# mLSTM cell and multiplicative FFN: the sign of high words on ScalarE, transposes of k, q and y moved from TensorE to VectorE and DRAM

## The chip, the cores and the metric

The kernel runs on one core of a Trainium2 chip. The metric is the device time of one execution in microseconds (us). The engines are PE (TensorE; PEld is its weight load, which overlaps the matmuls), DVE (VectorE), ACT (ScalarE), POOL (GpSimd) and SP (SyncE, which here only issues DMAs). [...]

## The reference, cut to what matters

For every batch (4) and head (8) an mLSTM cell runs over 768 time steps with a head size of 40; its output, 3072 tokens by 320, goes through a feed-forward block.

```python
for t in range(S):                                   # S = 768
    m_new  = max(f_gate + m, i_gate)
    C = exp(f_gate + m - m_new) * C + exp(i_gate - m_new) * outer(v, k)
    n = exp(f_gate + m - m_new) * n + exp(i_gate - m_new) * k
    y[t] = sigmoid(o_gate) * (C @ q) / max(abs(n @ q), 1)
x = y as (3072, 320)
out = (((x @ w1) * (x @ w2)) @ w3) @ w_out           # w1, w2: 320 x 1024; w3: 1024 x 1024; w_out: 1024 x 320
```

The four weights arrive as 64-bit floats, the rest as 32-bit floats. The kernel itself turns each weight into 32 bits, from its low and its high word.

## The kernel before, in words

**Units.** Time is cut into pieces of 128 steps, and a unit is one such piece of one batch: 6 x 4 = 24 units. Four units (one of each batch) are a group of 512 tokens of the feed-forward block. The main loop (L568) has 30 steps, s = 0 to 29. Step s runs the cell of unit s (its scores and its addition to the state, together with the output of unit s-1: `quarter_work`, L308), and beside it the feed-forward work of earlier units: "ups" (x @ w1 times x @ w2, `up` L521 and `up_rest` L534), "downs" (`ffn_out`, L544) from step 17 on, and in steps 10 to 17 one piece each of w3 @ w_out (`w3_mm`, L248), which is folded into one matrix.

**Weights.** `fetch` loads 64-bit words into `raw`; ScalarE scales the high word (`scale`, L171); VectorE puts the 32-bit number together in five instructions (`to_f32`, L175, lines 184 to 188), of which L185 fetches the sign. For w3 a sixth instruction turns the tile (L237). 34 such conversions are spread over steps 0 to 15 (`n_cvt`, L563).

**Transposes.** TensorE needs k, q and y with the token along the free dimension. For units 0 to 16 `turn` (L281) does k and q with eight 128x128 transposes on TensorE (tile `pt`) and two ScalarE copies out of PSUM (L295). For units 17 to 23 `load_turned` (L125) loads k and q in another arrangement, eight DMAs in all, into `turned_in`, one pair of buffers in the tile `gates`, and VectorE turns them by two 32x32-block transposes (L287). Units of that kind load no plain q. For y, `twice` (L385) has GpSimd copy the last 64 columns once more, and `x_trans` (L388) does three transposes on TensorE (tile `px`) and one ScalarE copy into `xT` (L396).

**Order.** All matmuls and transposes are held in the order in which they are recorded (`in_order`, L82). In a step this is: `pt`, `px` of unit s-3, `wp`, the downs, the ups, their rest (64-row matmuls), and then the cell: output of unit s-1, state product, and last the scores of unit s, which need kT and qT of unit s. On the other engines the tile framework's scheduler orders the instructions at build time; `tc.issue_after` marks some as not to be placed before another. PSUM has four rotating banks (`mps`, L75) for all but the cell, and the cell has one tile, which a step can write again only when VectorE has read it (`outputs`, L362, lines 366 and 370).

## Time and profile before

| | before |
|---|---|
| time, median of 3 runs | 486.15 us (486.0 to 486.35) |
| profiled execution, its own time | 483.81 us |
| span of that execution | 482.1 us |
| mean granted TensorE clock | 0.982 |
| busy: PE, DVE, ACT, POOL | 454.6, 259.9, 146.8, 86.6 us |
| DMA | 45.72 MB, mean 95 GB/s |

The span runs from the first to the last instruction; 1.7 us of the execution lie around it. In the timeline a step can be told by the tile `cell`: steps 12 to 15 take 16.77 us each, step 17 (one piece of w3 @ w_out and two downs) 24.51 us, and steps 18 to 23 20.2 us each. Durations of matmuls are modelled, so for TensorE the starts are read, and not the ends.

### The profile page before, as it was taken

What the parts mean: (1) busy time and instruction counts of PE and PEld (TensorE: products, weight loads), DVE (VectorE), ACT (ScalarE), POOL (GpSimd) and SP (SyncE); (2) the same over time, 40 slices, a digit from 0 to 9 for tenths busy, and PEclk for the clock granted to TensorE, in tenths of its full rate; (3) what the DMA queues carried; (4) which work ended last, traced back from release to release, by engine and by line L of the source; (5) the groups of instructions that cost most, each with busy time, mean ns of one, the idle gap of its engine ahead of it and who ended that gap; (6) DMA issues with size and microseconds to landing.
All of it is one profiled execution on the core that took longest, in us unless ns stands there. A gap on an engine that the chain in (4) does not pass through costs nothing.

```text
span 482.1 us, 12855 instructions
## 1 busy us (share of the span) xinstructions
PE 454.6 (94%) x5402; PEld 365.6 (76%) x5402; DVE 259.9 (54%) x526; ACT 146.8 (30%) x399; POOL 86.6 (18%) x165
## 2 busy tenths in 40 slices
PE   3868999799999999999999999999999998999997
PEld 2757877678878888788878787787877877778864
DVE  7797798989886968887451533614325033011110
ACT  3644545443442353354331321311101111011011
POOL 5442322520220322213220211201000000000000
PEclk9995999989999999999999999999999999999999
DMA  8999977599698656433350623324020000000001
GB/s 183 166 166 200 194 139 137 114 203 191 125 189 135 127 127 148 94 66 57 77 132 15 141 57 96 66 81 110 3 82 16 14 27 3 29 14 16 1 14 41
DMA packets 116185, 45.72 MB, mean 95 GB/s; under 512 B 96736, under 2 KB 107168, under 8 KB 116128
## 3 DMA queue, kind: packets, MB, share of 16 engines
q1 hardware_dynamic: 112528, 40.88, 43.4%
q10 hardware_dynamic: 3600, 4.03, 2.4%
q8 instruction: 42, 0.69, 0.6%
q14 instruction: 15, 0.12, 0.1%
HBM read 40.86 MB, written 4.03 MB: 93 GB/s over the span
## 4 chain that ended last, share of the span: by engine, by line
PE 81%; issue 7%; DVE 7%; POOL 2%; DMA 1%; ACT 1%; ACTq 0%; SPq 0%; POOLq 0%; DVEq 0%
PE pa L90 23%; PE po L90 22%; PE pb L90 16%; PE cell L90 9%; PE wp L90 7%; PE pt L93 2%; DVE h L370 1%; PE px L93 1%; PE ub L90 1%; POOL pw L278 1%; DVE o_in L380 1%; DVE h L366 1%; DMA raw<-in_moe_w_out_dram 1%; POOL state L305 1%; DMA gates<-in_i_gate_dram 1%
## 5 line engine op out<-in xcount | busy, mean ns | idle before, releaser
L542 DVE TENSOR_TENSOR ab<-pb,a_sb 128x512 f32<-128x512 f32 x48 | 33.0, 689 | 162.1 <-ACT a_sb L541 162.0
L90 PE MATMUL po<-w3o,ab 128*128 128x320 f32 x384 | 105.4, 433 | 1.3 <-DVE h L370 1.3
L90 PEld LDWEIGHTS po<-w3o,ab 128*128 128x128 f32 x384 | 72.2, 190 | 30.7 <-issue 1.5
L90 PE MATMUL pa<-xT,w 128*128 128x256 f32 x384 | 92.5, 384 | 0.9 <-ACT xT L396 0.6
L90 PE MATMUL pb<-xT,w 128*128 128x256 f32 x384 | 90.8, 379 | 0.0
L90 PEld LDWEIGHTS pa<-xT,w 128*128 128x128 f32 x384 | 73.3, 193 | 14.1 <-ACT xT L396 1.0
L90 PEld LDWEIGHTS pb<-xT,w 128*128 128x128 f32 x384 | 72.9, 190 | 10.3 <-DVE ab L542 0.4
L541 ACT ACTIVATE a_sb<-pa 128x512 f32<-128x512 f32 x48 | 28.6, 595 | 151.3 <-PE pb L90 151.3
L90 PE MATMUL pa<-xT,wr 64*64 64x256 f32 x384 | 47.0, 383 | 0.0
L90 PE MATMUL pb<-xT,wr 64*64 64x256 f32 x384 | 47.0, 383 | 0.0
L305 POOL TENSOR_TENSOR state<-state,decay 128x164 f32<-128x164 f32 x40 | 19.6, 495 | 146.9 <-PE cell L90 91.5
L278 POOL TENSOR_SCALAR_AFFINE_SELECT pw<-pw 64x512 f32<-64x512 f32 x48 | 35.5, 740 | 47.8 <-ACT pw L276 46.2
L276 ACT ACTIVATE pw<-pw,aT 128x64 f32<-128x64 f32 x160 | 40.7, 338 | 8.1 <-DMA pw<-U_d 8.1
L90 PEld LDWEIGHTS pa<-xT,wr 64*64 64x64 f32 x384 | 25.8, 133 | 16.8 <-issue 7.8
L90 PE MATMUL wp<-wo,w3T 128*128 128x320 f32 x128 | 35.9, 433 | 0.1
L90 PEld LDWEIGHTS cell<-vbuf,pw 64*64 64x64 f32 x768 | 27.5, 141 | 6.1 <-issue 1.9
L549 ACT COPY o_sb<-po 128x320 f32<-128x320 f32 x24 | 10.2, 423 | 67.9 <-PE po L90 63.6
L90 PEld LDWEIGHTS wp<-wo,w3T 128*128 128x128 f32 x128 | 23.7, 190 | 9.1 <-PE px L93 0.3
L90 PE MATMUL cell<-vbuf,pw 64*64 64x41 f32 x768 | 27.4, 231 | 2.2 <-issue 1.3
L386 POOL COPY y<-y 128x64 f32<-128x64 f32 x24 | 7.1, 296 | 108.1 <-DVE y L382 104.2
L90 PEld LDWEIGHTS pb<-xT,wr 64*64 64x64 f32 x384 | 25.8, 133 | 0.0
L346 DVE TENSOR_TENSOR pw<-cell,pw 128x512 f32<-128x512 f32 x24 | 16.4, 684 | 15.3 <-PE cell L90 15.2
(89 smaller groups left out, 514.0 us busy)
## 6 DMA issues: line engine op xcount, KB each, us to landing
raw<-in_moe_w_dram SPq DMA_DIRECT2D x64, 128.0 KB, 3.2
pw<-U_d SPq DMA_DIRECT2D x40, 128.0 KB, 3.6
kbuf<-in_k_dram SPq DMA_DIRECT2D x24, 160.0 KB, 4.4
vbuf<-in_v_dram SPq DMA_DIRECT2D x24, 160.0 KB, 5.0
o_in<-in_o_gate_dram SPq DMA_DIRECT2D x24, 160.0 KB, 4.0
out_dram<-o_sb ACTq DMA_DIRECT2D x24, 160.0 KB, 1.9
raw<-in_moe_w_dram SPq DMA_DIRECT2D x7, 512.0 KB, 5.9
qbuf<-in_q_dram SPq DMA_DIRECT2D x17, 160.0 KB, 4.8
```

The costliest lines, as they stand in the source:

```text
L90: in_order(nc.tensor.matmul(out, lhsT=lhsT, rhs=rhs, start=start, stop=stop))
L93: in_order(nc.tensor.transpose(out, in_, ident[0:n, 0:n]))
L276: nc.scalar.activation(out=pw[:, h, :], in_=src[:, h, :], func=AF.Exp, bias=aT[:, c, b * H + h:b * H + h + 1])
L278: nc.gpsimd.affine_select(out=pw[r], in_=pw[r], compare_op=OP.is_ge, fill=0.0, base=0, pattern=[[0, H], [1, L]], channel_multiplier=-1)
L305: nc.gpsimd.tensor_tensor(out=new, in0=old, op=OP.mult, in1=decay[:, b * NP:(b + 1) * NP, 2 * c + x:2 * c + x + 1] .to_broadcast([P, NP, D1]))
L346: first_read = nc.vector.tensor_tensor(out=pv, in0=ss, in1=pv, op=OP.mult)
L366: nc.vector.tensor_tensor(out=h.rearrange("p (n two) d -> p two n d", two=2), in0=pi, in1=gT[:, c, hs].rearrange("p (n two) -> p two n", t ...
L370: nc.vector.tensor_tensor(out=h[r], in0=ph[x], in1=h[r], op=OP.add)
L386: nc.gpsimd.tensor_copy(out=y_t[n][:, DM:DM + REM], in_=y_t[n][:, KF * P:DM])
L541: nc.scalar.mul(out=a_sb, in_=pa, mul=UP ** -2)
L542: nc.vector.tensor_tensor(out=ab_t[gr][j][:, fs[0]:fs[-1] + 1, t0:t0 + a_sb.shape[-1]], in0=pb, in1=a_sb, op=OP.mult)
L549: nc.scalar.copy(out=o_sb, in_=po)
```

## The change

Three things are changed.

1. The sign of a weight's high word is brought to its place by ScalarE: the scaling becomes a parametric ReLU with a slope of 2^32 for negative numbers, so that the shift by three on VectorE leaves the sign bit set or clear, and L185 goes.
2. `N_DVE` is 10 in place of 17: k and q of units 10 to 16, too, are loaded by `load_turned` and turned by VectorE.
3. From unit 15 on (`NY`; the sixteenth unit) y is sent to a DRAM tile by four DMAs (`send`), read back in another arrangement by four more (`get_back`), and turned by one VectorE transpose (`x_turn`). `twice` and `x_trans` are not called for these nine units. All the DMAs are issued by SP.

```diff
-    N_DVE = 17
+    N_DVE = 10
...
+    NY = 15
     KC = KF + 1
+    y_d = [dram.tile([P, 4, KC, 32], FP, name=f"y_d{n}") if n >= NY else None for n in range(NU)]
...
     def scale(raw):
         hi = raw[:, :, 1].bitcast(FP)
-        nc.scalar.mul(out=hi, in_=hi, mul=2.0 ** -111)
+        nc.scalar.activation(out=hi, in_=hi, func=AF.Prelu, scale=2.0 ** -111, alpha=2.0 ** 32)
...
         V.tensor_scalar(out=t, in0=hi, scalar1=3, scalar2=None, op0=OP.logical_shift_left)
-        V.scalar_tensor_tensor(out=t, in0=hi, scalar=0x80000000, in1=t, op0=OP.bitwise_and, op1=OP.bitwise_or)
         V.tensor_scalar(out=r, in0=t, scalar1=0xFF800000, scalar2=None, op0=OP.bitwise_and)
...
+    def send(n):
+        y = y_t.pop(n)
+        for cc in range(KF):
+            nc.sync.dma_start(out=y_d[n][:, :, cc, :], in_=y[:, cc * P:(cc + 1) * P].rearrange("t (i c) -> t i c", c=32))
+        for i in range(0, 4, 2):
+            nc.sync.dma_start(out=y_d[n][:, i:i + 2, KF, :], in_=y[:, KF * P:DM].rearrange("t (i c) -> t i c", c=32))
+    back_t = {}
+    def get_back(n):
+        back_t[n] = sb.tile([P, 4, KC, 32], FP, name="yb", tag="yb", bufs=1)
+        for i in range(4):
+            nc.sync.dma_start(out=back_t[n][32 * i:32 * (i + 1)].rearrange("r m k c -> r m (k c)"),
+                              in_=y_d[n][:, i].rearrange("(m r) k c -> r m (k c)", r=32))
+    def x_turn(n):
+        gr, j = divmod(n, GT)
+        if j == 0:
+            x_t[gr] = ffn.tile([128, KC, TG], FP, name="xT", tag="xT")
+        nc.vector.transpose(out=x_t[gr][:, :, j * P:(j + 1) * P].rearrange("c k (m r) -> c k m r", r=32),
+                            in_=back_t.pop(n).rearrange("r m k c -> r k m c"))
...
-        if 0 <= s - 2 < NU:
+        if NY <= s - 2 < NU:
+            send(s - 2)
+        elif 0 <= s - 2 < NY:
             twice(s - 2)
         if N_DVE <= s + 1 < NU:
             load_turned(s + 1)
-        while turned < min(s - 2, NU):
+        if NY <= s - 2 < NU:
+            get_back(s - 2)
+        while turned < min(s - 2, NY):
             x_trans(turned)
             turned += 1
...
-        if len(now) == 1 and turned == s - 2 < NU:
+        if len(now) == 1 and turned == s - 2 < NY:
...
         with tc.issue_after(gated.ins) if gated else nullcontext():
+            if NY <= s - 2 < NU:
+                x_turn(s - 2)
             if N_DVE <= s + 1 < NU:
                 turn(s + 1)
```

## The prediction

> **What bounds the kernel now.** First the page's slices: where an engine is full, and at what TensorE clock.

> ```profile
> PE   3868999799999999999999999999999998999997
> DVE  7797798989886968887451533614325033011110
> PEclk9995999989999999999999999999999999999999
> ```

> TensorE is full from slice 8 (97 us) to the end. Before that it has holes, VectorE is at eight tenths, and the clock dips twice. Then the stretches, step by step (columns: length, busy PE, PEld, DVE, ACT, POOL, clock, DMA share, GB/s):

> ```profile
> 157.33:174.10 16.77, 16.77 (x220) 13.81 (x221) 13.69 (x28) 6.93 (x20) 3.56 (x6) 1.00 0.58 119
> 241.19:265.70 24.51, 24.51 (x244) 19.02 (x245) 7.53 (x15) 5.45 (x15) 3.24 (x7) 1.00 0.31 72
> 33.80:35.20 1.40, 0.04 (x4) 0.00 (x0) 1.30 (x4) 0.69 (x1) 0.24 (x1) 0.98 1.04 109
> 35.20:36.70 1.50, 0.00 (x0) 0.00 (x0) 1.35 (x2) 0.00 (x0) 0.00 (x0) 0.50 0.87 122
> 96.70:100.20 3.50, 3.19 (x9) 2.46 (x9) 3.24 (x9) 2.90 (x11) 0.00 (x0) 0.53 1.27 170
> ```

> Step 12 (first line) has no TensorE idle time, so what is taken from TensorE there is won in full, provided that nothing new makes it wait. The last three: where TensorE idles for a few us, its clock halves. Then the chain that ended last (start, length):

> ```profile
> 174.10 1.02 PE pt L93 x8
> 175.45 4.31 PE wp L90 x16
> 241.19 0.48 PE px L93 x3
> ```

> The transposes are on it. Last the timelines of VectorE and TensorE around the end of step 17, where k and q are already turned by VectorE, and three waits:

> ```profile
> 246.16 1.11 DVE L287 STREAM_TRANSPOSE kT<-gates 128x512 f32<-128x512 f32 x1
> 247.11 1.09 DVE L287 STREAM_TRANSPOSE qT<-gates 128x512 f32<-128x512 f32 x1
> 263.19 0.69 DVE L542 TENSOR_TENSOR ab<-pb,a_sb 128x512 f32<-128x512 f32 x1 [14.99 <-ACT a_sb L541]
> 264.06 0.69 DVE L542 TENSOR_TENSOR ab<-pb,a_sb 128x512 f32<-128x512 f32 x1 [0.17 <-ACT a_sb L541]
> 264.95 0.26 PE L90 MATMUL cell<-qT,kT 40*64 40x64 f32 x2
> 265.63 0.55 PE L93 MATMUL px<-ident,y 128*128 128x128 f32 x3
> 266.01 1.24 PE L90 MATMUL po<-w3o,ab 128*128 128x320 f32 x4
> 95.82 0.66 PE L93 MATMUL pt<-ident,qbuf 128*128 128x128 f32 x4 [2.57 <-DVE ab L542]
> 407.92 4.28 PE L90 MATMUL po<-w3o,ab 128*128 128x320 f32 x15 [1.29 <-DVE h L370]
> ```

> The reader is to see that step 17 turns k and q at its start (246 us), 17 us before the scores want them at 264.95, and that the second `ab` ends only 0.2 us before the scores start.

> [...] the transpose at 95.82 waited 2.57 us behind an `ab` that stood behind conversions. [...] The trace agrees on the half (0.50) and on the grid (the changes at 35.2, 96.7 and 100.2 us lie whole multiples of 3.42 us apart), but the drop at 35.2 us came only 1.4 us into a gap[...]. [...] the trace has a single load, of 1283 ns, and the changed program also holds one.

> **The change part by part.** "Step" is the loop's s; the sums are made on the profiled execution (span 482.1, time 483.81 us).

> *Sign.* 34 instructions of L185 leave VectorE: 32 of 668 ns in the mean and 2 of 852, 23.1 us together (0.69 on a wide tile, 0.49 on w_out's narrow ones). They pay only where TensorE waits for VectorE. Up to step 5 it doesn't: VectorE idles 0.7 to 1.1 us before each L346, for the cell. In step 5 VectorE is late by 2.7 us (L346 starts at 68.78, its scores end at 66.1); two conversions fewer by 0.69 each bring L346 to 67.40, and step 6 loses another 0.69 + 0.49 and its lateness. What was late there on TensorE goes: 0.17 us (bank of `pb`, step 6) and 1.07 us (`pt` of q at 80.23). In step 7 the cell then ends 1.24 us earlier, at 91.35; L346 runs at 78.4, `y` ends 5.45 later as before (80.69 to 86.14), at 83.85, three conversions take 8.96 less 3 sign instructions (0.84 + 0.49 + 0.49, and gaps) = 7.05 and end at 90.9. The changed order puts three quarters of a fourth conversion (1.2 us) ahead of the first `ab`: it ends at 92.75, the second at 93.85, where `pa` had to wait until 97.18. That is 3.3 us. The wait before it shrinks from 2.57 to 0.8 us, so the halved clock at 96.7 should not come: `pa` took 3.38 where it takes 1.73, 1.65 us more. Together **-4.9** (between -2, if stalls in loads take the place of the conversions, and -6.5, if step 9 gains too). The activation itself stays at its 0.63 us.

> *k and q of units 10 to 16.* Off TensorE go eight `pt` a step: step 17 without its downs is 24.51 - 8.61 = 15.90, against 16.77: 0.87 a step. ScalarE loses two copies of 0.59, off the path. Added are 2 transposes of 1.1 us on VectorE, eight DMAs less one q load on SP. VectorE has room in sum: 13.69 - 2 x 0.67 + 2.2 = 14.6 us a step. What decides is where they stand. The built program lists for steps 11 to 15

> ```
> ...  ab  ab  kT<-gates  qT<-gates  pw<-cell (L346)
> ```

> and for step 10 `ab ab`, a whole w3 conversion, then kT, qT; in step 16 qT stands before the second `ab`, and from step 17 on both follow `y`, as at 246.16. The `ab`s wait for this step's ups, so kT and qT can't start before them; the scores, the last matmuls of the same step, wait for both; behind the scores stands the whole next step. Priced on step 17: second `ab` at 264.06, kT 0.60 later (the spacing at which VectorE follows a 0.69 us instruction), qT 0.95 after it and 1.10 long: 266.71, and 0.05 for the semaphore. The scores would start at 264.95: **1.81 us of stall a step**. Steps 12 to 15: -0.87 + 1.81 = +0.94, four times = +3.8. Step 11: 17.71 against 17.85 (it held 0.85 us of idle issue): -0.1. Step 10: the conversion (0.45 + 0.46 + 0.73 + 0.73 + 0.64 = 3.0) comes on top: 15.90 + 4.8 = 20.7 against 17.07: +3.6. Step 16: -0.9. Together **+6.4**. The turned loads come in time: each is issued after the last turn, some 16 us before the next, and lands in 2.5 us.

> *Clock.* The gap of 4.8 us in step 10 must halve the clock for about a window: half of 3.42 = +1.7. The gaps of 1.81 us, behind 1.7 us of small cell matmuls, look like the window that dropped at 35.2 us[...]. The trace shows no such gap; between 0 and 5 x 1.7 I take 2.5 x 1.7: **+4.2**.

> *y of units 15 to 23.* Off TensorE go three `px` in steps 18 to 26: 266.01 - 265.63 = 0.38 each. In step 25 the first down also waits for `h` until 407.92, since `px` takes the free bank before it; without `px` the down takes that bank, at 406.08: 1.84. Sum 8 x 0.38 + 1.84 = **-4.9**. Added: one VectorE transpose of some 0.9 us (between L237's 0.71 and L287's 1.1; not seen with this shape), beside 13 idle us a step; and eight DMAs a unit. x of a unit is wanted one step or more after it is turned; `send` plus `get_back` take perhaps 6 us after `y`, and x_turn stands a step (20 us) later. So nothing; if they took more than 20 us, kT and qT behind x_turn would stall the scores.

> Sum: -4.9 + 6.4 + 1.7 + 4.2 - 4.9 = **+2.5**: a profile of some 486.3 us, and 486.15 + 2.5 = **488.7 us** for the median, which lies 2.3 above this profiled execution.

> **The rivals.**
> 1. *The clock holds.* A gap of 1.3 us at 406.6 and one of 1.17 at 61.0 left it at 1.00. If 1.81 does too: +2.5 - 4.2 = -1.7, and without step 10's, -3.4: **483.6**, faster. It decides at two dips in five steps: with none or one dip the sum is negative or zero. Chance 0.21.
> 2. *Every step dips*, or two windows each: 5 x 1.7 and more, +6.7 and beyond: **493**. Chance 0.16.
> 3. *A turned load is late.* SP also carries eight `raw` DMAs a step (9.0 us in step 12) and the turned loads now wait for VectorE in the midst of them. Late by 2 us in six steps: **500**. Against it: 16 us of room. Chance 0.07.
> 4. *The turns don't stall* (the scores find them ready): -4.9 - 7.3 - 4.9 = -17, **469**. Against it: the listed order. Chance 0.05.

> **How the numbers follow.** The forecast has 0.51. Its own range is 486 to 491; with rivals 1 and 2, and the bounds of the sign's gain, 483 to 495.5; some 0.14 stay outside. Against 486.15 a measurement tells 0.2% (1 us) from nothing: faster, rival 1 mostly, rival 4: 0.22; same, the forecast's low end: 0.15; slower: 0.63.

> **What would show it.** Right: TensorE waits for DVE qT (L287's new line) in steps 10 to 15, 1.8 us each and 4.8 in step 10; dips of the clock in those slices; steps of 17.7 us or more; no `pt` there; `pa` of step 8 some 5 us earlier; steps 18 to 23 of 19.8 us. Wrong: waits of the transposes for DMA, ScalarE table loads, or steps 11 to 15 at 15.9 us.

## The result, and the profile after

The changed kernel takes **489.13 us**, the median of 4 runs (488.72 to 490.29), against 486.25 us for the kernel before in the same comparison (4 runs, 486.0 to 487.29): a ratio of **1.0059**, 95% interval 1.0035 to 1.0083. It is slower by 2.9 us; the prediction was 488.7. (Ratios leave out executions more than 1.5% above the fastest of their kernel; below, that concerns two of the six of sign and y without k and q, and four of the twenty of the sign alone, while medians are of all.) The profiled execution took 488.72 us; its span is 487.0 us, its mean TensorE clock 0.951.

First the page's slices of the changed kernel, to be laid beside those of before:

```profile
PE   3898999899959889889899999999999999999997
DVE  6666598988776878858851416246053241211110
PEclk9655799999979999899999999999999999999999
```

TensorE, full from slice 8 to the end before, now has a hole in slice 11 (5; the slices count from 0, each is 12.2 us) and several slices of 8 up to slice 19, and the clock has two new dips there, in slices 11 and 16. Those are steps 10 to 15. The first slices hold the low clock longer; that comes back below.

The stretches from the end of one step's cell to the next, for steps 10 to 12, 14 and 16 to 18 of the changed kernel (length, busy PE, PEld, DVE, ACT, POOL, clock, DMA share, GB/s):

```profile
121.00:142.87 21.87, 16.54 (x213) 13.42 (x213) 16.76 (x31) 6.13 (x16) 5.38 (x9) 0.92 0.75 138
142.87:162.23 19.36, 17.86 (x212) 14.20 (x213) 13.72 (x25) 5.42 (x15) 4.24 (x6) 0.91 0.59 125
162.23:179.83 17.60, 16.11 (x212) 13.03 (x213) 13.95 (x25) 5.42 (x15) 3.90 (x6) 1.00 0.68 141
...
197.42:216.72 19.30, 17.80 (x214) 14.03 (x213) 13.73 (x25) 5.42 (x15) 4.24 (x6) 0.91 0.64 129
...
234.32:250.23 15.91, 15.91 (x214) 12.96 (x213) 10.53 (x20) 6.60 (x22) 4.55 (x7) 1.00 0.55 104
250.23:274.74 24.51, 24.51 (x244) 19.02 (x244) 7.50 (x15) 5.94 (x17) 4.21 (x8) 1.00 0.47 102
274.74:294.66 19.92, 19.92 (x225) 15.70 (x225) 7.99 (x16) 4.30 (x13) 2.93 (x6) 1.00 0.61 116
```

Step 12 (third line) was 16.77 us with no TensorE idle time; it is 17.60 with 1.49 us idle (length less busy PE). Step 14 has the same idle time, a clock of 0.91, and is 1.70 us longer. Step 16 has no idle time and is 0.87 us shorter than before. VectorE is busy 14 of 17.6 us, so it isn't full.

What TensorE waits for, in the changed kernel (sum in us, times, longest):

```profile
PE cell L90 <- DVE qT L288: 12.8, 6, 5.3
...
PE pt L93 <- DVE ab L567: 1.9, 1, 1.9
```

Six waits for the turn of q in steps 10 to 15, one of them 5.3 us. And the timelines around the end of step 11, VectorE first, then TensorE:

```profile
158.03 0.69 DVE L567 TENSOR_TENSOR ab<-pb,a_sb 128x512 f32<-128x512 f32 x1 [3.51 <-ACT a_sb L566]
158.89 0.69 DVE L567 TENSOR_TENSOR ab<-pb,a_sb 128x512 f32<-128x512 f32 x1 [0.17 <-ACT a_sb L566]
159.50 1.08 DVE L288 STREAM_TRANSPOSE kT<-gates 128x512 f32<-128x512 f32 x1
160.44 1.04 DVE L288 STREAM_TRANSPOSE qT<-gates 128x512 f32<-128x512 f32 x1
```

```profile
159.37 0.67 PE L90 MATMUL cell<-vw,kbuf 64*64 64x41 f32 x30
161.54 0.69 PE L90 MATMUL cell<-qT,kT 40*64 40x64 f32 x32 [1.50 <-DVE qT L288]
162.16 0.55 PE L93 MATMUL px<-ident,y 128*128 128x128 f32 x3
162.54 4.47 PE L90 MATMUL wp<-wo,w3T 128*128 128x320 f32 x16
```

VectorE idles 3.51 us ahead of the first `ab`, while the turns stand behind both `ab` in its list; then come both `ab`, then kT and qT, and the scores start 0.06 us after qT ends (161.48, 161.54). TensorE was done with the state product at about 160.0. So VectorE kept to its list through those 3.51 us, although the turns' inputs were there: their loads were issued by 145.8 us and took at most 3.2 us to land. No turn of k or q waits for its load anywhere in this profile.

The table sums the two profiled executions (483.81 and 488.72 us; spans 482.1 and 487.0). A step ends where its cell's scores end.

| stretch | before | after | difference | predicted |
|---|---|---|---|---|
| start to end of step 5 | 66.16 | 68.91 | +2.75 | 0 |
| steps 6 to 9 | 56.25 | 52.09 | -4.16 | -4.9 |
| step 10 | 17.07 | 21.87 | +4.80 | +3.6, and the first part of 1.7 for the clock |
| step 11 | 17.85 | 19.36 | +1.51 | -0.1, and the rest of that 1.7 |
| steps 12 to 15 | 67.08 | 72.09 | +5.01 | +3.8, and up to 4.2 for the clock |
| steps 16 and 17 | 41.29 | 40.42 | -0.87 | -0.9 |
| step 18 to the end | 216.40 | 212.26 | -4.14 | -4.9 |
| sum | 482.1 | 487.0 | +4.9 | +2.5 |

### The profile page after: what moved, and what is told of

It is laid out like the page before. It is cut to its first block, busy times and chain, and to the rows that moved or that the text cites. A ratio compares the mean times of both kernels' runs of the same rounds, so it can differ in the third digit from the quotient of the medians.

```text
span 487.0 us, 12836 instructions
## 1 busy us (share of the span) xinstructions
PE 454.2 (93%) x5319; PEld 364.0 (75%) x5319; DVE 258.7 (53%) x515; ACT 135.1 (28%) x376; POOL 86.8 (18%) x156
## 4 chain that ended last, share of the span: by engine, by line
PE 81%; issue 6%; DVE 6%; ACT 2%; POOL 2%; DMA 1%; SPq 0%; DVEq 0%; POOLq 0%; ACTq 0%
PE pa L90 24%; PE po L90 22%; PE pb L90 17%; PE wp L90 8%; PE cell L90 7%; DVE kT L288 1%; PE px L93 1%; PE pt L93 1%; DVE qT L288 1%; DMA kbuf<-in_k_dram 1%; PE ub L90 1%; ACT pw L277 1%; ACT a_sb L566 1%; DVE h L371 1%; POOL pw L279 1%
## 5 line engine op out<-in xcount | busy, mean ns | idle before, releaser
L90 PE MATMUL po<-w3o,ab 128*128 128x320 f32 x384 | 106.2, 435 | 0.0
L90 PEld LDWEIGHTS po<-w3o,ab 128*128 128x128 f32 x384 | 72.1, 190 | 30.1 <-issue 0.4
L90 PE MATMUL pa<-xT,w 128*128 128x256 f32 x384 | 92.9, 386 | 0.6 <-ACT xT L421 0.6
L90 PE MATMUL pb<-xT,w 128*128 128x256 f32 x384 | 91.4, 381 | 0.0
L90 PEld LDWEIGHTS pa<-xT,w 128*128 128x128 f32 x384 | 73.4, 193 | 13.7 <-ACT xT L421 1.0
L90 PEld LDWEIGHTS pb<-xT,w 128*128 128x128 f32 x384 | 73.5, 191 | 10.4 <-ACT kT L296 0.3
L90 PE MATMUL pa<-xT,wr 64*64 64x256 f32 x384 | 47.0, 383 | 0.0
L90 PE MATMUL pb<-xT,wr 64*64 64x256 f32 x384 | 47.0, 383 | 0.0
L90 PE MATMUL wp<-wo,w3T 128*128 128x320 f32 x128 | 38.8, 460 | 0.0
L90 PEld LDWEIGHTS pa<-xT,wr 64*64 64x64 f32 x384 | 25.8, 132 | 16.8 <-issue 7.8
L90 PE MATMUL cell<-qT,kT 40*64 40x64 f32 x768 | 20.0, 239 | 14.8 <-DVE qT L288 12.8
L90 PEld LDWEIGHTS wp<-wo,w3T 128*128 128x128 f32 x128 | 25.6, 206 | 10.1 <-issue 2.2
L90 PEld LDWEIGHTS cell<-vbuf,pw 64*64 64x64 f32 x768 | 28.4, 145 | 4.9 <-PE px L93 1.3
L90 PE MATMUL cell<-vbuf,pw 64*64 64x41 f32 x768 | 28.5, 235 | 0.9 <-PE px L93 0.9
L90 PEld LDWEIGHTS cell<-qT,kT 40*64 40x64 f32 x768 | 16.5, 147 | 15.8 <-DVE qT L288 13.5
```

The lines of the kernel that those rows point to most:

```text
L90: in_order(nc.tensor.matmul(out, lhsT=lhsT, rhs=rhs, start=start, stop=stop))
```

## The experiments

Theory: kT and qT stand behind both `ab` in VectorE's list, the scores wait for them, and after some of these gaps TensorE's clock halves (from 1.00 to 0.50, at 139.6 and 197.6 us in the changed kernel); sign and y both gain. Rivals: turned loads or SyncE's queue are late; VectorE is too full; the cost comes from y or the sign; the clock is beside the point. The kernel before was timed with each group of runs (medians 486.13, 484.14, 484.86 and 485.57 us), so ratios are compared, not times. The tables of steps come from each run's profiled execution.

### Each part alone

**k and q alone**, on the kernel before:

```diff
-    N_DVE = 17
+    N_DVE = 10
```

> The kernel before with only the turns of k and q on VectorE from the 11th unit on; sign and y as before. Theory (the cell waits for turns that stand behind both ab products on VectorE, and the clock halves after some of these gaps): steps 10 to 16 cost what they cost in the changed kernel, +10.4 us by the two traces, and the conversion ahead of the turns of step 10 is one operation of 0.6 us longer: 496 to 498 us. Rival (the loads of the turned k and q are late, or VectorE is too full): the same total, but the cell of steps 11 to 15 would be released by a DMA, or VectorE would be busy up to the turns with conversions. Rival (k and q are harmless and the cost comes from y or the sign): within 1 us of 486.

Measured: 499.18 us, ratio 1.0263 (1.0238 to 1.0288), +12.8 us on 486.25. This part alone is the loss, and larger than expected. Steps 12, 13 and 15 are 17.60 us, to the hundredth as in the changed kernel, and step 14 again 19.30. The surplus sits in step 10, 24.89 us where the changed kernel has 21.87: half of it is a longer wait for qT (6.83 us instead of 5.33), and half is a wait at the start of the step, of `wp` for the turned w3, that the changed kernel doesn't have. TensorE's two lines of this run:

```profile
126.24 4.54 PE L90 MATMUL wp<-wo,w3T 128*128 128x320 f32 x16 [1.29 <-DVE w3T L237]
148.24 1.13 PE L90 MATMUL cell<-qT,kT 40*64 40x64 f32 x32 [6.83 <-DVE qT L287]
```

VectorE's list between the second `ab` and kT holds a whole conversion, and with the sign still on VectorE it is longer by L185 (1.10 us); before that, a turn of w3 stands between the two `ab`. No turn of k or q waits for its load in this run either. So in step 10 the sign's removal also pays within what k and q cost, and there the two are not additive.

**Sign and y without k and q**, on the changed kernel:

```diff
-    N_DVE = 10
+    N_DVE = 17
```

> The changed kernel with k and q turned by VectorE only from the 18th unit on, as before: sign and y alone. Theory: sign -4.2 us and y -4.1 us by the two traces: 477 to 479 us; 480 to 481 if the +2.8 us of the first five steps belongs to the change and not to the moment at which the clock's windows fall. Rival (the DMAs of y or the queues are what costs): 484 or more.

Measured: 477.23 us, ratio 0.9787 (0.9741 to 0.9833). By the ratio it is faster by 10.4 us on 486.25, with a wide interval (8.1 to 12.6 us); the medians of all executions (477.23 and 486.13) are 8.9 us apart; in the profile steps 12 to 16 are 16.77 us as before, and steps 18 to 23 are 19.92. The rival that y's transfers cost is out.

**The sign alone**, on the kernel before:

```diff
-        nc.scalar.mul(out=hi, in_=hi, mul=2.0 ** -111)
+        nc.scalar.activation(out=hi, in_=hi, func=AF.Prelu, scale=2.0 ** -111, alpha=2.0 ** 32)
...
-        V.scalar_tensor_tensor(out=t, in0=hi, scalar=0x80000000, in1=t, op0=OP.bitwise_and, op1=OP.bitwise_or)
```

> The kernel before with only the sign taken by the parametric ReLU, one VectorE operation less in each conversion. Theory: worth the 4.2 us that steps 6 to 8 showed, where the second ab product waits behind conversions: 486.1 - 4.2 = 482 us, 481 to 483; the prediction had 4.9. Rival (those steps are bound by the raw words' arrival or by TensorE): within 1 us of 486.

Measured: 480.81 us, ratio 0.9923 (0.9900 to 0.9946), -3.7 us on 486.25. Its steps 6 to 9 take 52.10 us against 56.25 before: the 4.2 us are there again.

**y alone**: the changed kernel with the sign and `N_DVE = 17` put back.

> The kernel before with only y sent through DRAM from the 16th unit on. Theory: eight steps at 0.28 us, since the first po takes 0.19 us longer where no px stands ahead of it, and the 1.76 us of the wait for h in step 25: 486.1 - 4.0 = 482 us, 481 to 483. Rival (each px is worth its whole 0.48 us on TensorE): 8 x 0.48 + 1.76 = 5.6, 480.5. Rival (the queue of SyncE is late with what stands behind the eight transfers): 486 or more.

Measured: 481.35 us, ratio 0.9933 (0.9911 to 0.9955), -3.3 us on 486.25. Steps 18 to 23 are 19.92 us against 20.20: 0.28 each, not the 0.38 of the prediction nor the 0.48 of the rival.

The three parts add up to +12.8 - 3.7 - 3.3 = +5.8 us; together they are +2.9. The difference of 2.9 has intervals of over a microsecond on every term. The 3.0 us by which step 10 is shorter with the sign gone agree with it, but k and q together with the pair of sign and y give +12.8 - 10.4 = +2.4 (+3.9 with the medians' 8.9), with little or nothing missing. So that the parts are not additive is read from step 10 of the two traces; the times don't decide it.

### The order on VectorE

**The `ab` behind the turns.** An edge for the order alone, that gives no semaphore:

```diff
+    turned_last = []
+    def after_turn(ins, i=-1):
+        if len(turned_last) >= -i:
+            tc.add_manual_dep(ins.ins, turned_last[i].name, mybir.DependencyInfo(
+                mybir.DependencyClass.NoSync, mybir.DependencyReason.DATA), reason="after_turn")
...
-                nc.vector.transpose(out=dst[n].rearrange("i p (r f) -> i p f r", f=4),
-                                    in_=src[:, 32:TB].rearrange("i (p f d) -> i p f d", p=NP, f=4)[:, :, :, 0:32])
+                turned_last.append(nc.vector.transpose(out=dst[n].rearrange("i p (r f) -> i p f r", f=4),
+                                    in_=src[:, 32:TB].rearrange("i (p f d) -> i p f d", p=NP, f=4)[:, :, :, 0:32]).ins)
...
-        nc.vector.tensor_tensor(out=ab_t[gr][j][:, fs[0]:fs[-1] + 1, t0:t0 + a_sb.shape[-1]], in0=pb, in1=a_sb, op=OP.mult)
+        after_turn(nc.vector.tensor_tensor(out=ab_t[gr][j][:, fs[0]:fs[-1] + 1, t0:t0 + a_sb.shape[-1]], in0=pb, in1=a_sb, op=OP.mult))
```

> The changed kernel with one edit: each ab product has an order-only edge to the turn of q for its step, so that in steps 10 to 16 VectorE's order is kT, qT, ab, ab; TensorE, ScalarE and SyncE keep their order. Theory: the stall of 1.7 us goes in steps 11 to 15, where nothing else stands ahead of the turns, and those steps fall to 15.9 us like step 16; step 10 keeps its stall, since a whole conversion stands ahead there: 489.1 - (1.5+0.9) - 3 x 1.7 - 3.4 = 478 us, 477 to 480. Rival (turned loads late): the order doesn't matter, 489. Rival (VectorE too full): the ab products now wait, TensorE waits for their banks: 483 or more.

Measured: 478.21 us, ratio 0.9841 (0.9815 to 0.9868). Steps 12 to 15 are 15.90 us; step 10 keeps its 21.92. Both as the theory had it: the same loads, the same work on VectorE, only the places changed.

**The conversions behind the turns too.** The run before, and

```diff
-        V.tensor_scalar(out=t, in0=hi, scalar1=3, scalar2=None, op0=OP.logical_shift_left)
+        after_turn(V.tensor_scalar(out=t, in0=hi, scalar1=3, scalar2=None, op0=OP.logical_shift_left), -3)
```

> As the run before, and the conversions too get an edge: those of a step stand behind the turn of q for that step, so that the turns come right behind y in every step, or behind the two conversions at most. Theory: steps 10 to 16 all fall to about 15.9 to 16.2 us, no stall is left and no clock dip with it: 489.1 - 10.45 - 7 x 0.9 = 472 us, 470.5 to 474. Rival (turned loads late): 489, with the turns waiting for a DMA. Rival (conversions put off come late): w3's products wait for their turned tile, 2 us in some steps, 476 to 484.

Measured: **470.23 us, ratio 0.9684 (0.9659 to 0.9709)**, 15.4 us faster than the kernel before and 18.2 us (on 486.25) faster than the changed one, though its three parts are all there. The timeline of VectorE in step 12 of this run:

```profile
160.39 1.10 DVE L288 STREAM_TRANSPOSE kT<-gates 128x512 f32<-128x512 f32 x1
161.35 1.09 DVE L288 STREAM_TRANSPOSE qT<-gates 128x512 f32<-128x512 f32 x1
165.34 0.69 DVE L567 TENSOR_TENSOR ab<-pb,a_sb 128x512 f32<-128x512 f32 x1 [2.91 <-ACT a_sb L566]
166.21 0.69 DVE L567 TENSOR_TENSOR ab<-pb,a_sb 128x512 f32<-128x512 f32 x1 [0.17 <-ACT a_sb L566]
```

and its steps 9, 10 and 11 (the first still has its `pt` for unit 9):

```profile
107.68:120.15 12.47, 12.47 (x205) 10.78 (x205) 11.09 (x24) 5.91 (x16) 2.11 (x4) 1.00 0.99 204
120.15:136.05 15.90, 15.90 (x212) 12.95 (x213) 14.02 (x28) 4.94 (x13) 3.03 (x7) 1.00 1.00 183
136.05:151.94 15.89, 15.89 (x212) 12.93 (x213) 13.10 (x25) 6.46 (x20) 5.46 (x9) 1.00 0.83 172
```

The turns now fill time in which VectorE idled: 2.91 us of it are still left ahead of the first `ab`. Steps 10 to 16 are all 15.9 us, without TensorE idle time and at full clock; the line "cell <- DVE qT" is gone from the waits. ScalarE and SyncE run the same lists as in the changed kernel, and TensorE's order is kept, so a late load would have stayed late: the rival of late turned loads is out for the changed kernel. So is the rival of conversions that come late when put off.

### The clock

**q turned twice**: 1.04 us more in the gap, on the changed kernel.

```diff
-                nc.vector.transpose(out=dst[n].rearrange("i p (r f) -> i p f r", f=4),
+                for _ in range(2 if name == "qT" and n > 10 else 1):
+                    nc.vector.transpose(out=dst[n].rearrange("i p (r f) -> i p f r", f=4),
                                     in_=src[:, 32:TB].rearrange("i (p f d) -> i p f d", p=NP, f=4)[:, :, :, 0:32])
```

> The changed kernel with the turn of q done twice into the same tile for units 11 to 23: 1.04 us more of VectorE between the ab products and the scores in steps 11 to 15, and more time in which TensorE idles; from step 17 on it lies in idle time. Theory, the stall alone: 489.1 + 5 x 1.04 = 494.3 us, and no more, if the clock doesn't answer to the longer gap. Theory, with the clock: the gap grows from 1.5 to 2.5 us, and nearly every such step loses 1.7 us to a halved clock, instead of one or two of the five: 489.1 + 5.2 + 3 or 4 x 1.7 = 499.5 to 501. Rival (the cell waits for something else than the turn of q, which the profile only names): 489.

Measured: 502.55 us, ratio 1.0373 (1.0343 to 1.0402), 15.3 us more than the changed kernel on 486.25 (13.2 between the two profiled executions). The longer stall itself is 5.2 us of it in steps 11 to 15 and about 1.1 in step 16, where the scores now wait for qT as well (0.92 us). Steps 13 and 14 of this run, and TensorE's timeline at the end of step 12:

```profile
183.47:203.88 20.41, 17.80 (x212) 13.90 (x213) 13.92 (x26) 5.50 (x15) 3.83 (x6) 0.92 0.62 128
203.88:224.29 20.41, 17.79 (x213) 13.96 (x213) 13.92 (x26) 5.50 (x15) 3.82 (x6) 0.92 0.61 122
```

```profile
182.78 0.69 PE L90 MATMUL cell<-qT,kT 40*64 40x64 f32 x32 [2.61 <-DVE qT L288]
183.40 0.55 PE L93 MATMUL px<-ident,y 128*128 128x128 f32 x3
183.78 6.16 PE L90 MATMUL wp<-wo,w3T 128*128 128x320 f32 x16
```

17.60 + 1.04 = 18.64 would be the stall alone; each step is 1.77 us above that, and `wp` takes 6.16 instead of 4.47 us. Read in stretches of 0.1 us, the clock falls to 0.50 at 163.4, 183.9, 204.4, 224.9 and 245.4 and comes back 3.4 to 3.5 us later each time: five gaps, five drops. They lie 20.5 us apart, while a step is 20.41.

The clock's changes lie on a grid: in each of ten traces (before, changed, and eight of the experiments) they are whole multiples of 3.413 us apart, to 0.01 us. In the changed kernel it changes at 16.71, 54.25, 139.59, 146.42, 197.62 and 201.03 us, which is 11, 25, 2, 15 and 1 times 3.413 from one to the next, and between them it is 1.00 or 0.50. Six times 3.413 is 20.48. So the five drops are hardly five independent cases; the step has fallen in with the grid.

With gaps of 1.5 us, whether the clock dropped went with the position in that grid. There are ten such gaps in two profiled executions, five in the changed kernel and five in k and q alone, and in each execution only the gap of step 13 is followed by a drop. There the clock changes 0.2 to 0.3 us after the scores end (197.61 us against 197.43; 204.29 against 204.03). After the other eight the next moment of the grid, counted in steps of 3.41 us from the changes seen, comes 0.7 to 1.5 us after the scores, and the clock held. In the changed kernel the five stretches of 3.41 us that end there take in the gap whole or nearly so, and TensorE is busy 1.92 to 2.07 us in each; but the one before the drop at 197.61 holds 102 matmuls, little but small ones around the gap, and the other four 39 to 71, with large ones of `wp` in their last part. With q turned twice the moment comes 0.4 to 0.7 us after the scores, the stretch holds most of a gap of 2.6 us, and all five dropped. That the clock goes by what TensorE does in such a stretch is the author's reading of three executions, and isn't shown: no run moved a gap within it on purpose.

**The gap filled**: the run above, and ahead of the scores of units 11 to 16

```diff
+            if N_DVE < n < NY + 2:
+                fill = mps([128, 2, 2 * P], "fill")
+                for i in range(8):
+                    mm(fill[:, i % 2, :], ident, w1[:, 0, 0:2 * P], start=True, stop=True)
             kT, qT, pw = kT_t.pop(n), qT_t[n], u_t[n]
```

> The run with q turned twice, and in its steps 11 to 16 eight products of the identity with 256 columns of w1 (about 0.22 us each, into a PSUM tile that nobody reads) ahead of the scores, so that TensorE works through most of the 2.6 us in which it idled. The scores still wait for the same turn of q. Theory (the halved clock comes of the idle gap): the five drops of 1.77 us after the gaps of steps 11 to 15 go, the stall stays: 502.6 - 5 x 1.77 = 493.7 us, a ratio of 1.019 to the kernel before, with steps 12 to 15 at 18.6 us. Rival (the 1.77 us are a late w3T or the memory traffic behind the gap, and the clock is only beside it): 502 or more, ratio 1.037.

Measured: 500.31 us, ratio 1.0330 (1.0297 to 1.0363). The filler was wrong in size: 0.22 us is one 128x256 instruction of `pa` (1.73 us for eight in the changed kernel), but each product is two instructions of some 0.24 us each, so eight took 3.8 us of TensorE and ended after qT. Steps 12 to 16 are 19.7 us, 15.9 plus the filler, with the clock at 1.00: no drop, but the comparison in time is spoilt.

**Five products on the changed kernel itself** had the same fault:

> The changed kernel itself with five such products ahead of the scores in steps 11 to 16. Theory: every stall of 1.7 us stays, so steps 11 to 15 are 17.6 us each, and what goes is the halved clock after these gaps: one of five in the profiled execution, 2.5 of five by the prediction. 1.7 to 4.2 us less than the changed kernel, a ratio of 0.997 to 1.002 to the kernel before. Rival (the clock takes nothing in these steps): 1.006.

Measured: 491.57 us, ratio 1.0140 (1.0100 to 1.0180): a miss. 2.4 us of filler in a gap of 1.5 us make steps 12 to 16 18.4 us each, all at full clock. What the clock takes in these steps over many executions can't be read from it.

**Five products, q turned twice**, 2.4 us of filler in a gap of 2.6:

```diff
-                for i in range(8):
+                for i in range(5):
```

> The run with q turned twice and the gap filled, with five filler products instead of eight: the profile of that run showed each of them as two instructions of 0.24 us, so eight were 3.8 us, longer than the gap of 2.6 us, and five are 2.4 us. The scores then wait for the turn of q again, as without fillers. Theory (the halved clock comes of the idle gap): steps 12 to 16 at 17.60 + 1.04 = 18.65 us instead of 20.41, wp at 4.3 to 4.5 us instead of 6.2: a ratio of 1.019 to the kernel before. Rival (late w3T or memory traffic): 20.4 us a step, ratio 1.037.

Measured: 495.37 us, ratio 1.0227 (1.0186 to 1.0269). Its steps 13 and 14, and TensorE at the end of step 12:

```profile
178.50:197.28 18.78, 18.46 (x223) 14.86 (x223) 14.54 (x26) 5.52 (x15) 4.16 (x6) 1.00 0.66 134
197.28:216.27 18.99, 18.48 (x224) 14.88 (x223) 14.71 (x26) 5.39 (x15) 3.57 (x6) 1.00 0.65 132
```

```profile
174.87 2.43 PE L90 MATMUL fill<-w,ident 128*128 128x256 f32 x10
177.81 0.69 PE L90 MATMUL cell<-qT,kT 40*64 40x64 f32 x32 [0.51 <-DVE qT L289]
178.44 0.55 PE L93 MATMUL px<-ident,y 128*128 128x128 f32 x3
178.82 4.47 PE L90 MATMUL wp<-wo,w3T 128*128 128x320 f32 x16
```

More work for TensorE, and the kernel is faster: 18.8 to 19.0 us a step against 20.41, `wp` back at 4.47 us, the clock at 1.00 in all of these steps, while the scores still wait for the turn of q. With q turned twice, then, the halved clock comes of TensorE's idling, not of a late w3T or of memory traffic. Steps 12 to 15 stay 0.1 to 0.3 us above the expected 18.65, which isn't explained. The ratio came out above the expected 1.019, which lies just inside the interval; the rival's 1.037 lies outside.

### Further in the same direction

**y through DRAM from the 10th unit on**, with the turns first (`NY = 9`):

> The run with the turns ahead of products and conversions, and y through DRAM from the 10th unit on instead of the 16th. Theory: six more steps lose their px, 0.3 to 0.5 us each, and VectorE, which has over 2.5 us of idle time per step there, hides the extra turn of y: 470.2 - 2.4 = 468 us, 467 to 469. Rival (SyncE's queue holds up the raw words of w3 and the loads behind eight more transfers a step, or VectorE is late with kT and qT): 471 to 480.

Measured: 469.04 us, ratio 0.9680 (0.9649 to 0.9710), no different from the 0.9684 without it. In the profile steps 12 to 14 fall from 15.90 to 15.62 us, but step 15 rises to 16.02: 1.2 us from step 9 to step 23 in all, half of what was expected and below what these intervals tell apart. In step 15 the rival shows in small: the turn of q is late with its load, and TensorE waits 0.20 us for that turn.

```profile
213.91 1.12 DVE L288 STREAM_TRANSPOSE qT<-gates 128x512 f32<-128x512 f32 x1 [1.99 <-DMA gates<-in_q_dram]
```

The run without early y has no such wait; whether y's transfers in SyncE's list make the load late wasn't tested.

**k and q from the 10th unit on** as well (`N_DVE = 9`):

> The run with the turns first and y early, with k and q on VectorE from the 10th unit on instead of the 11th. The turns of that unit come in step 8, behind two conversions and right ahead of the ab products of step 9, whose 12.5 us VectorE nearly fills. Theory (a turn is worth about 0.9 us where VectorE has time left, and costs a wait where it has not): 0.9 us faster if they end before the second ab is due, 468; if not, the pa or the scores of step 9 wait 1 to 2 us, 470 to 471. Rival (the loads of turned k and q collide with the raw words of w3 this early): 472 or more.

Measured: 472.07 us, ratio 0.9724 (0.9685 to 0.9763), not faster. VectorE's timeline at the end of step 9 of this run:

```profile
118.60 0.71 DVE L238 STREAM_TRANSPOSE w3T<-w 128x512 f32<-128x512 f32 x1
119.24 1.05 DVE L288 STREAM_TRANSPOSE kT<-gates 128x512 f32<-128x512 f32 x1
120.15 1.05 DVE L288 STREAM_TRANSPOSE qT<-gates 128x512 f32<-128x512 f32 x1
121.23 1.29 DVE L567 TENSOR_TENSOR ab<-pb,a_sb 128x512 f32<-128x512 f32 x2
```

There is no idle time ahead of anything and no wait for a load, which was the rival: here VectorE is full with conversions up to the turns. TensorE waits 1.8 us for qT, the clock is 0.50 from 122.46 to 125.87 us, step 9 is 13.64 instead of 12.47 and step 10 17.59 instead of 15.90. Order helped only where VectorE had idle time to put the turns in.

## Why the prediction was right, step by step

*The stall in steps 11 to 15* was right in place, cause and size: 1.81 us a step predicted; 17.60 - 15.90 = 1.70 measured. The step without stall, 15.90, was hit to the hundredth by step 16 and by the run with the turns first.

*Step 10* was right in mechanism and short in size. The conversion ahead of kT was put at 3.0 us from spacings elsewhere; from 135.87 to 139.75 us it took 3.88, because two of its operations ran 1.10 and 1.02 us, not 0.73. TensorE waited 5.33 us and not 4.8. The VectorE lines (L186 to L189 are the conversion):

```profile
135.26 0.69 DVE L567 TENSOR_TENSOR ab<-pb,a_sb 128x512 f32<-128x512 f32 x1 [0.17 <-ACT a_sb L566]
135.87 0.42 DVE L186 TENSOR_SCALAR ex<-raw 128x512 uint32<-128x512 uint32 x1
...
136.93 1.10 DVE L188 SCALAR_TENSOR_TENSOR ma<-raw,ma 128x512 f32<-128x512 uint32 x1
138.06 1.02 DVE L189 TENSOR_TENSOR w<-ex,ma 128x512 f32<-128x512 f32 x1
...
139.75 1.04 DVE L288 STREAM_TRANSPOSE kT<-gates 128x512 f32<-128x512 f32 x1
```

*The clock.* In step 10 it was +1.7 for one stretch of the grid, an estimate; in the kernel before the clock was 0.50 from 96.60 to 100.01 us and `pa` took 3.38 us there, not 1.73. In the changed kernel it fell at 139.6 and came back at 146.4, two stretches of 3.41 us. The first lies half in the idle time; together they cost 0.44 us in the scores (1.13 instead of 0.69) and 1.76 in step 11, 2.2 us. After the five gaps of steps 11 to 15, 2.5 drops were predicted, and the profiled execution has one, at 197.6 us after step 13: 1.70 us instead of 4.2. This term was the one most mis-sized: that half of the gaps would be followed by a drop was the author's estimate, which the trace of before didn't show, and eight of the ten gaps seen in two executions held. The chain of waits of the changed kernel shows where the low clock is paid:

```profile
141.74 1.13 PE cell L90 x32
142.87 0.83 PE px L93 x3
143.70 5.71 PE wp L90 x16
```

Of five gaps of 1.5 us one was followed by a drop, at the same place in the grid in both executions (0.2 and 0.3 us after the scores). So after a gap of 1.5 us it fell twice in ten, and with q turned twice, after gaps of 2.6 us, anew in each of five steps. How many drops the other executions of the changed kernel have isn't known, since only one was profiled.

*The sign*: -4.9 predicted, -4.16 in the profile, -3.7 in its own run. The chain was as described: the wait of q's `pt` for `ab` fell from 2.57 to 1.88 us, not to 0.8, and `pa` behind it ran at full clock (1.99 instead of 3.38 us). The 34 activations took 0.63 us each in the mean in both kernels, with one table load of 1283 ns in each. Not seen was the gain of 3.0 us in step 10 when k and q are moved as well; the prediction listed the shorter conversion there, and so had that half of it in the sum of k and q without saying so. One reading was loose, without consequence for the sum: up to step 5 VectorE idles before the `L346` of four steps (0.7 to 1.7 us), but not before that of step 1, at 27.77 us.

*y*: -4.9 predicted, -4.14 in the profile, -3.3 in its own run. The wait in step 25 went as predicted: from the end of the cell to the next `pa` it is 8.72 us (413.15 to 421.87) where it was 10.53 (406.08 to 416.61), -1.81 for 1.84. The eight steps were mis-sized: 0.28 each, for 0.38. The first `po` is followed by the next `pa` after 8.62 us where `px` stood ahead of it (266.01 to 274.63, before), and after 8.72 where not (274.67 to 283.39, after), so that 0.1 of the 0.38 us is needed anyway. The turn on VectorE takes 0.57 us, for the estimate of 0.9, and delays nobody. From the end of the last unit's `y` to its turn, which waits for the loads, it is 6.7 us (416.54 to 423.23), for the estimate of 6.

*The sum.* On the profiled executions it is +4.9, not +2.5. The terms above, put right, give -4.16 + 10.45 - 4.14 = +2.15; the rest, +2.75, arises in the first five steps, where the prediction had nothing. Nothing ties it to the change. Stretches of 8 us there, the kernel before first, then the changed one (columns as above):

```profile
20.00:28.00 8.00, 7.36 (x186) 6.72 (x186) 7.53 (x11) 5.45 (x20) 4.16 (x5) 1.00 0.79 121
28.00:36.00 8.00, 4.46 (x152) 3.84 (x148) 7.07 (x16) 3.75 (x12) 2.88 (x5) 0.95 1.02 181
```

```profile
20.00:28.00 8.00, 7.87 (x162) 7.01 (x160) 4.97 (x7) 4.56 (x17) 4.09 (x5) 0.50 0.84 128
28.00:36.00 8.00, 7.56 (x156) 6.92 (x152) 7.01 (x15) 3.64 (x12) 3.13 (x5) 0.50 1.19 191
```

Before, the clock was 1.00 and 0.95 in them, after 0.50. But ten of the kernels here, all with the new sign, run the same lists up to step 8. This one stays at the low clock from 16.7 to 54.3 us, others fall at 26.2, 34.9, 35.3 or 37.9, and their step 5 ends anywhere from 65.35 to 69.99 us, in the main later where the clock comes back for good later (46.7 us for the earliest end, 55.8 for the latest). With the old sign the three ends are 66.16 (before), 68.41 (k and q alone) and 69.07 (y alone), within that range. This execution drew a late end (68.91) and the profiled one of before an early one (66.16). Medians, in which such draws should weigh less, give +2.9 against the +2.5 of the sum. It was hit with terms that missed in both directions: the clock was put 2.0 us too high (2.2 + 1.7 measured, 5.9 predicted), the gains of sign and y 1.5 us too high. So the mechanism was right, and that the total came within half a microsecond is in part luck; by the prediction's own sum, one drop in five steps, which is what this profile has, would have made the change worth nothing.

*Rivals.* "The clock holds" (483.6) needs no drop; there were three stretches of 3.41 us at 0.50 in steps 10 to 15. "Every step dips" (493) came true only with a longer gap. The late load (500) and turns that don't stall (469) are settled by the run with the turns first: 470.2 is what this change gives when the order is right.

## What to carry to other kernels

Work moved to an engine with room cost nothing here only where its place in that engine's list was early enough; ask what stands ahead of it, and what that waits for. Here both `ab` of the same step stood ahead of work whose inputs had been there for long, and edges for the order alone turned +0.6% into -3.2%. Where a scheduler decides at build time, read its list after every change of this kind; and count an idle gap of the matrix engine twice, once for its length (1.5 us a step here) and once for the clock that may halve after it (1.7 us more where it fell to 0.50).
